# Column-normalised attention folded into a two-layer MLP: scores in two row halves, single-block first tiles, and GpSimd in the sum of squares

## Chip, core and metric

The kernel runs on one core of one Trainium2 chip. The metric is device time in microseconds (us) of one launch; the kernel before was timed in three runs, with a median of 1041.66 us (1041.51 to 1043.06).

## The reference, cut to what is computed

```python
def _attn_ref(q, k, v, tau):                     # q, k, v: (1, 6016, 256) float32
    qn = q / (np.linalg.norm(q, axis=1, keepdims=True) + 1e-06)
    kn = k / (np.linalg.norm(k, axis=1, keepdims=True) + 1e-06)
    s = kn.transpose(0, 2, 1) @ qn / tau          # 256 x 256: channels against channels
    s = s - s.max(-1, keepdims=True)
    a = np.exp(s)
    a /= a.sum(-1, keepdims=True) + 1e-09
    return (v @ a).astype(np.float32)

def _moe_ref(x, w_in, w_out):                     # w_in 256 x 2048, w_out 2048 x 256, float64
    h = x @ w_in
    g = h * (1.0 / (1.0 + np.exp(-1.702 * h)))
    return (g @ w_out).astype(np.float32)

def _moe2_ref(x, w_in, w_out):
    h = x @ w_in
    return (np.maximum(0.01 * h, h) @ w_out).astype(np.float32)
# out = _moe2_ref(_moe_ref(_attn_ref(q, k, v, tau), moe weights), moe2 weights)
```

## The kernel before

The norms run over the 6016 rows, so the attention is a 256 x 256 matrix of scores between channels, and a softmax over its rows. The kernel never forms v @ a: it folds a into the first layer's weights (`fold`, L478) and multiplies v by those. Exact float32 products are made of three float32r products (`terms`, L88): each operand is split into a high and a low part (`halves`, L94: ScalarE copies the high part, VectorE subtracts), and high x high, high x low and low x high are added up. The weights come as float64 words and are turned into float32 by a chain of small steps, `convert` (L193), driven by a generator: each `go_on(n)` (L296) emits the next n steps, so it is the place of `go_on` in the program that places this work in the queues of VectorE and ScalarE.

The whole order is written out by hand: each engine executes its instructions in the order of the program.

1. Front (L301 to L404). q and k come in tiles of `rows` (L318: 1, 1, 2, ten times 4, 2 and 1 blocks of 128 rows), eight tiles ahead, q on SP's DMA queue and the first three tiles of k on ScalarE's. Six small products `warm` (L370) precede them. For each block the TensorE makes both halves of the scores, `s_ps[kc]`, one product of 256 columns each, with q as the weights, so that the rows of the scores are channels of q. ScalarE squares the tile and VectorE adds the squares into `acc` (`add_squares`, L343). `norms` (L354) sums `acc` over the partitions ahead of the last three blocks' products.
2. Chain (L417 to L475). The inverse norms of q and tau go into two diagonal matrices `dq`; ScalarE copies the scores (`st`), and eight instructions at L442 multiply the transposed scores by `dq`. Then a row maximum, `Exp` with the inverse norm of k as its scale, four transposes at L463, and the split of the exponentials into `eth` and `etl`.
3. First block of v (L406 to L504 and L666 to L704). `transpose_v` turns v's first 1024 rows, `fold(0)` makes the first slice of folded weights `wa[0]`, and `hidden_first` makes the hidden products of slice f, for both 512-row halves u and for both w_in halves s; `emit_y` multiplies the activated tiles by `wo`, one pair of tiles behind.
4. The remaining blocks and the second layer (`step`, L706, and `last_step`, L763), at a steady pace that the change doesn't touch.

PSUM has eight banks: y00, y10, y01, y11 and h0 to h3. A bank is used under several names one after the other, and a new use waits for the readers of the old one: `nrm` is h0, `et` is h1, the scores are y00 and y10, and `hidden_first` writes bank h(2s+u).

Of the kernel before, what the change touches and what calls it, by code (L numbers as in the profile page):

```python
# [7 lines left out]
F32 = mybir.dt.float32  # L8
# [9 lines left out]
def tile_kernel(  # L18
# [31 lines left out]
    P = 128  # L50
# [28 lines left out]
    ones = small(const, 1, "ones")  # L79
# [34 lines left out]
    with tc.manual_schedule():  # L114
# [15 lines left out]

        make_identity(nc, ident)
        nc.gpsimd.memset(ones, 1.0)
# [60 lines left out]
        def convert(key):  # L193
# [28 lines left out]
            if name == "wo":  # L222
                hi, lo = (wo[f][:, s].rearrange("p k c -> p (k c)") for s in range(2))
                nc.vector.tensor_copy(hi, flat)
                yield
                subtract(lo, flat, hi.bitcast(F32))
                yield
                return
            if name == "wi":
                wi = early.tile([P, 2, BLK], F32R, tag="ws", name="wi", bufs=2)  # L230
                nc.vector.tensor_copy(wi[:, 0], flat)
                yield
                subtract(wi[:, 1], flat, wi[:, 0].bitcast(F32))
                ready[f] = wi
                yield
                return
# [66 lines left out]
        sc = front.tile([P, KC, C], F32, name="sc")  # L303
        taub = small(front, 1, "taub")
        rtau = small(front, 1, "rtau")
        dq = front.tile([P, KC, P], F32, name="dq")
        root = small(front, 4, "root")
        rr = small(front, 4, "rr")
        rn = small(front, 4, "rn")
        mx = small(front, KC, "mx")  # L310
        rk = small(front, KC, "rk")
        st = front.tile([P, KC, C], F32, name="st")
        den = small(early, KC, "den")
        rden = small(early, KC, "rden")
        nc.vector.memset(acc, 0.0)


        rows = [1, 1, 2] + [4] * 10 + [2, 1]  # L318
# [19 lines left out]
        V_TILE = 7  # L338
        CONVERT = {last - 1: 5}
# [3 lines left out]
        def add_squares(j):  # L343
            t, n = qk(j), rows[j]
            sq = front.tile([P, 2, 4, C], F32, tag="sq", name="sq", bufs=2)
            nc.scalar.activation(out=sq[:, :, :n, :], in_=t[:, :, :n, :], func=AF.Square)
            step = 2 if j < last - 1 else 1
            for r in range(0, n, step):
                m = min(step, n - r)
                add(acc[:, :, :m, :], acc[:, :, :m, :], sq[:, :, r:r + m, :])  # L350
            if j == last - 2:
                add(acc[:, :, 0, :], acc[:, :, 0, :], acc[:, :, 1, :])

        def norms():  # L354
            for i in range(2):
                for kc in range(KC):
                    nc.tensor.matmul(  # L357
                        nrm[:, 2 * i + kc:2 * i + kc + 1],
                        lhsT=acc[:, i, 0, kc * P:(kc + 1) * P],
                        rhs=ones,  # L360
                        start=True,
                        stop=True,
                    )

        for j in range(AHEAD):
            load_qk(j)
            if j == 2:
                nc.scalar.preload_act_table(AF.Sqrt)

        warm = bank("h3")  # L370
        for _ in range(6):
            nc.tensor.matmul(warm[:, :P], lhsT=ident, rhs=ident, start=True, stop=True)
        for j in range(len(rows)):
            t, n = qk(j), rows[j]
            if j == last - 1:

                for i in range(last - 1, last + 1):
                    add_squares(i)
                norms()
            for r in range(n):  # L380
                for kc in range(KC):
                    nc.tensor.matmul(  # L382
                        s_ps[kc][:, :C],
                        lhsT=t[:, 0, r, kc * P:(kc + 1) * P],
                        rhs=t[:, 1, r, :],
                        start=(j == 0 and r == 0),
                        stop=(j == last and r == n - 1),
                    )
            if j < last - 1:
                add_squares(j)  # L390
            go_on(CONVERT.get(j, 0))
            if j + AHEAD <= last:
                load_qk(j + AHEAD)
            if j == V_TILE:
                for _ in range(3):
                    next_load()
# [6 lines left out]
            if j == last - 1:  # L403
                nc.vector.reciprocal(out=rtau, in_=taub)  # L404

        def transpose_v(c, tags):  # L406
            pts = [bank(tag) for tag in tags]
            for kc in range(KC):
                for i in range(BLK // P):
                    nc.tensor.transpose(  # L410
                        pts[kc][:, i * P:(i + 1) * P],
                        qk(V_TILE)[:, c, i, kc * P:(kc + 1) * P], ident,
                    )
            return pts


        nc.vector.tensor_scalar_add(rr, nrm[:, 0:4], 1e-35)  # L417
# [13 lines left out]

# [3 lines left out]
        for d in range(KC):  # L435
            nc.scalar.copy(st[:, d, :], s_ps[d][:, :C])
        go_on(2)

        sq_ps = [bank("h2"), bank("h3")]
        for kc in range(KC):  # L440
            for d in range(KC):
                nc.tensor.matmul(  # L442
                    sq_ps[kc][:, d * P:(d + 1) * P],
                    lhsT=st[:, d, kc * P:(kc + 1) * P], rhs=dq[:, d, :], start=True, stop=True,
                )
        vt0 = transpose_v(0, ("y01", "y11"))

        for kc in range(KC):
            row = sq_ps[kc][:, :C]
            nc.vector.tensor_reduce(out=mx[:, kc:kc + 1], in_=row, axis=AX.X, op=ALU.max)  # L450
            nc.vector.tensor_scalar(
                out=mx[:, kc:kc + 1], in0=mx[:, kc:kc + 1], scalar1=rk[:, kc:kc + 1], scalar2=-1.0,
                op0=ALU.mult, op1=ALU.mult,
            )
            nc.scalar.activation(  # L455
                out=sc[:, kc, :], in_=row, func=AF.Exp, bias=mx[:, kc:kc + 1],
                scale=rk[:, kc:kc + 1], accum_out=den[:, kc:kc + 1],
            )
        go_on(2)
        et = bank("h1")  # L460
        for kc in range(KC):
            for d in range(KC):
                nc.tensor.transpose(  # L463
                    et[:, d * C + kc * P:d * C + (kc + 1) * P], sc[:, kc, d * P:(d + 1) * P], ident
                )
        et3 = et.rearrange("p (d c) -> p d c", d=KC)
        nc.vector.tensor_copy(eth, et3)  # L467
        subtract(etl, et3, eth.bitcast(F32))
        nc.vector.tensor_scalar_add(rden, den, 1e-9)
        nc.vector.reciprocal(out=rden, in_=rden)  # L470
        for dst, src in ((xa[0], vt0[0]), (xbt, vt0[1])):
            halves(dst[:, 0, 0], dst[:, 1, 0], src)
        nc.scalar.preload_act_table(AF.Gelu_apprx_sigmoid)
        while 0 not in ready:
            go_on(1)  # L475


        def fold(f):  # L478

            wi = ready.pop(f).rearrange("p h (d n) -> p h d n", d=KC)  # L480
            pw = bank("h0" if f == 1 else "h3").rearrange("p (k n) -> p k n", k=KC)
            for kc in range(KC):
                c0 = slice(kc * P, (kc + 1) * P)
                for d in range(KC):
                    terms(pw[:, kc], (eth[:, d, c0], etl[:, d, c0]), (wi[:, 0, d], wi[:, 1, d]),
                          d == 0, d == KC - 1)
            raw = early.tile([P, 4, P], F32, tag="tp", name="raw")
            for kc in range(KC):

                nc.scalar.activation(  # L490
                    out=raw[:, 0::3] if kc == 0 else raw[:, 1:3],
                    in_=pw[:, kc].rearrange("p (s n) -> p s n", s=2), func=AF.Copy,
                    scale=rden[:, kc:kc + 1],
                )
# [4 lines left out]

        fold(0)  # L500
        vt1 = transpose_v(1, ("y00", "y10"))
        for dst, src in ((xa[0], vt1[0]), (xbt, vt1[1])):
            halves(dst[:, 0, 1], dst[:, 1, 1], src)
        go_on(4)  # L504
# [161 lines left out]
        def hidden_first(f):  # L666
# [5 lines left out]
            for u in range(2):  # L672
                hp = bank(f"h{2 * s + u}")
                for kc, x in enumerate((xa[0], xbt)):
                    terms(hp, (wa[g][:, 0, at[kc]], wa[g][:, 1, at[kc]]),
                          (x[:, 0, u], x[:, 1, u]), kc == 0, kc == KC - 1)
                act(1, h[:, u], hp)
            if f == NF:
                fold(1)
# [12 lines left out]
        for f in range(NF):  # L692
            for s in range(2):
# [7 lines left out]
                emit_y(len(pend) - 2)  # L701
# [183 lines left out]
```

## Time and profile before

| | |
|---|---|
| median of three runs | 1041.66 us |
| the profiled execution, its time and its span | 1043.86 us, 1042.0 us |
| mean granted TensorE clock over the span | 0.997 |
| TensorE busy | 1031.5 us, 99% |
| VectorE, ScalarE, GpSimd busy | 775.0, 589.9 and 0.7 us |
| TensorE's first score product | 4.07 us |
| the norms' products | 46.84 us |
| first hidden product | 58.32 us |
| hidden products of slice 2, first half, and their y done | about 88.1 us |

In the profile PE is the TensorE's matrix products, DVE is VectorE, ACT is ScalarE, POOL is GpSimd and SP the engine that issues DMAs. A float32 product shows as two instructions, so one block's product with one half of the scores ("a unit" below) is two rows. The ends of matmuls are modelled, so short waits of the TensorE hide in their durations: its real pace is read from the starts. [...]

### The profile page before, as it was taken

Reading aid. Unit: us, or ns where it says so; the run is one execution under the profiler, and the core shown is the slowest. Engines: PE = TensorE matmul, PEld = TensorE weight load, DVE = VectorE, ACT = ScalarE, POOL = GpSimd, SP = SyncE. Lnnn points to the kernel's source line nnn. Section 1 sums busy time; section 2 is a strip of 40 time slices with the busy share of each in tenths; the row PEclk is TensorE's granted clock in tenths of the full one; section 3 lists DMA queues with packets and bytes.
Section 4 is the critical chain, followed back from the end, with each engine's and each line's share of the span. In section 5 each row is a group of like instructions: output and inputs, shape, how many; then the busy total and the mean of one; then the engine's idle time right before and its main releaser. Section 6 shows DMA issues by size and latency. Waiting matters only on the chain.

```text
span 1042.0 us, 12633 instructions
## 1 busy us (share of the span) xinstructions
PE 1031.5 (99%) x4676; PEld 870.6 (84%) x4676; DVE 775.0 (74%) x1187; ACT 589.9 (57%) x864; POOL 0.7 (0%) x7
## 2 busy tenths in 40 slices
PE   8999999999999999999999999999999999999998
PEld 7878888888888888888998888888888888888997
DVE  6889868888888888888766667577567667676655
ACT  5465555666556666666556555555555555455453
POOL 0000000000000000000000000000000000000000
PEclk9999999999999999999999999999999999999999
DMA  9646423015224223212744002101200300300202
GB/s 361 234 126 167 129 65 91 10 31 150 92 68 110 98 76 103 89 56 96 263 167 152 1 1 42 41 1 19 63 1 9 73 1 1 76 1 1 41 1 36
DMA packets 120077, 81.82 MB, mean 79 GB/s; under 512 B 93392, under 2 KB 104400, under 8 KB 118736
## 3 DMA queue, kind: packets, MB, share of 16 engines
q1 hardware_dynamic: 115872, 80.04, 25.3%
q10 hardware_dynamic: 4144, 0.98, 0.4%
q8 instruction: 36, 0.59, 0.2%
q14 instruction: 25, 0.20, 0.1%
HBM read 55.05 MB, written 25.95 MB: 78 GB/s over the span
## 4 chain that ended last, share of the span: by engine, by line
PE 97%; DVE 1%; DMA 1%; issue 0%; ACT 0%; ACTq 0%; DVEq 0%
PE y L92 49%; PE h L92 44%; PE y L382 4%; DMA qk<-in_k_dram 1%; DVE gd L99 0%; PE h L442 0%; ACTq L330 0%; ACT raw L490 0%; ACT sc L455 0%; DVE ta L208 0%; PE h L357 0%; DVE ta L203 0%; DVE etl L99 0%; DVE eth L467 0%; DVE ta L212 0%
## 5 line engine op out<-in xcount | busy, mean ns | idle before, releaser
L92 PE MATMUL y<-gd,wo 128*128 128x512 f32 (+1 forms) x1248 | 296.5, 386 | 0.1
L92 PE MATMUL h<-xa,wa 128*128 128x512 f32 (+1 forms) x1152 | 276.5, 385 | 0.5 <-DVE wa L496 0.5
L92 PEld LDWEIGHTS y<-gd,wo 128*128 128x128 f32 x1248 | 233.8, 188 | 44.1 <-DVE gd L99 0.4
L92 PEld LDWEIGHTS h<-xa,wa 128*128 128x128 f32 x1152 | 216.2, 188 | 41.7 <-DVE wa L496 0.8
L92 PE MATMUL y<-g,wo 128*128 128x512 f32 (+1 forms) x1044 | 246.8, 385 | 0.0
L92 PEld LDWEIGHTS y<-g,wo 128*128 128x128 f32 x1044 | 196.0, 188 | 36.3
L92 PE MATMUL h<-xb,wa 128*128 128x512 f32 (+1 forms) x888 | 217.3, 385 | 0.0
L92 PEld LDWEIGHTS h<-xb,wa 128*128 128x128 f32 x888 | 166.7, 188 | 31.1
L99 DVE TENSOR_TENSOR tv<-tp,h 128x512 f32<-128x512 f32 (+1 forms) x88 | 59.3, 674 | 114.4 <-PE h L92 111.8
L99 DVE TENSOR_TENSOR cc<-tv,h 128x512 f32<-128x512 f32 (+1 forms) x176 | 116.0, 673 | 34.9 <-PE h L92 34.4
L96 DVE TENSOR_TENSOR gd<-cc,gd 128x1024 fp32r<-128x1024 f32 (+1 forms) x87 | 104.1, 1197 | 0.0
L722 ACT COPY tp<-h 128x512 f32<-128x512 f32 (+1 forms) x87 | 50.4, 580 | 93.2 <-PE h L92 92.6
L95 ACT CAST gd<-cc 128x1024 fp32r<-128x1024 f32 (+1 forms) x87 | 90.0, 1035 | 0.0
L516 ACT ACTIVATE cc<-cc 128x1024 f32<-128x1024 f32 (+2 forms) x49 | 50.3, 1027 | 38.9 <-DVE cc L99 38.9
L516 ACT ACTIVATE tt<-tt 128x512 f32<-128x512 f32 (+1 forms) x48 | 30.0, 625 | 72.4 <-DVE tt L99 72.4
L99 DVE TENSOR_TENSOR tt<-tv,h 128x512 f32<-128x512 f32 (+1 forms) x88 | 59.4, 675 | 9.9 <-DVE tv L99 0.9
L99 DVE TENSOR_TENSOR tt<-tt,h 128x512 f32<-128x512 f32 (+1 forms) x88 | 59.4, 675 | 9.2
L514 ACT ACTIVATE cc<-cc 128x1024 f32<-128x1024 f32 (+1 forms) x40 | 41.6, 1041 | 40.9 <-DVE cc L99 40.9
L99 DVE TENSOR_TENSOR g<-tt,g 128x512 fp32r<-128x512 f32 (+1 forms) x87 | 58.6, 673 | 7.2 <-ACT g L733 6.9
L514 ACT ACTIVATE tt<-tt 128x512 f32<-128x512 f32 (+1 forms) x40 | 24.9, 623 | 64.8 <-DVE tt L99 64.8
L99 DVE TENSOR_TENSOR g<-tp,g 128x512 fp32r<-128x512 f32 (+1 forms) x87 | 58.6, 674 | 0.0
L746 ACT CAST g<-tp 128x512 fp32r<-128x512 f32 (+1 forms) x87 | 53.2, 612 | 2.8
(97 smaller groups left out, 713.0 us busy)
## 6 DMA issues: line engine op xcount, KB each, us to landing
cv<-in_moe_w_in_dram SPq DMA_DIRECT2D x32, 256.0 KB, 3.2
cv<-in_moe_w_out_dram SPq DMA_DIRECT2D x16, 512.0 KB, 3.9
wa<-w2a SPq DMA_DIRECT2D x8, 896.0 KB, 4.7
qk<-in_q_dram SPq DMA_DIRECT2D x10, 512.0 KB, 9.9
qk<-in_k_dram SPq DMA_DIRECT2D x10, 512.0 KB, 10.0
x<-stg SPq DMA_DIRECT2D x5, 1024.0 KB, 4.6
stg<-x SPq DMA_DIRECT2D x5, 1024.0 KB, 5.2
out_dram<-o SPq DMA_DIRECT2D x80, 64.0 KB, 1.9
```

Of the source, the lines that this page charges most:

```text
L92: nc.tensor.matmul(dst, lhsT=w, rhs=x, start=start, stop=stop, skip_group_check=more)
L95: nc.scalar.copy(hi, raw)
L96: nc.vector.tensor_tensor(out=lo, in0=raw, in1=hi.bitcast(F32), op=ALU.subtract)
L99: nc.vector.tensor_tensor(out=out, in0=in0, in1=in1, op=op)
L382: nc.tensor.matmul(s_ps[kc][:, :C], lhsT=t[:, 0, r, kc * P:(kc + 1) * P], rhs=t[:, 1, r, :], start=(j == 0 and r == 0), stop=(j == last an ...
L514: nc.scalar.activation(out=out, in_=in_, func=AF.Gelu_apprx_sigmoid)
L516: nc.scalar.activation(out=out, in_=in_, func=AF.Prelu, alpha=0.01)
L722: nc.scalar.copy(tp, pa)
L746: nc.scalar.copy(g11[:, 0], tp)
```

## The change

- Tiles: six tiles of one block, one of two, nine of four, then two and one. Four tiles of k instead of three go by ScalarE's queue. The small products ahead multiply `ones` (now 128 x 128, set before `ident`) instead of `ident`.
- Squares: in the tiles of four blocks up to tile 14 VectorE adds three blocks and GpSimd the fourth, into an accumulator `accp` of its own (eight such adds). The last three tiles are squared and added q and k apart, then `accp` and the second half of `acc` are added in.
- Scores: k is the weight operand, so rows are channels of k. Tiles 0 to 13 make both halves; tiles 14 to 17 (11 blocks) only half 0 before the norms. The 11 products of half 1 come after the norms, in groups of 2, 4, 3 and 2 between the steps of the chain.
- Chain: instead of the copies `st` and the products at L442, `spread` sends the scaled inverse norms of q to all partitions with one product by `ones`; one VectorE instruction multiplies a half of the scores by it and takes the maximum. The chain runs once for each half. `fold(0)`, its scaling and its split are done by halves as well, and the first products of slice 0 on the first 128 channels of v (`first_products(0, ...)`) are put among them.
- Slice 0 of the first block: only the second 128 channels are left in `hidden_first`; its y products come right after the hidden products of both s (no longer one pair behind), with `fold(1)` between them.
- The high parts of `wi` 0 and 1 and of `wo` 0 are copied by ScalarE instead of VectorE.

The diff, cut to its core:

```diff
-    ones = small(const, 1, "ones")
+    ones = const.tile([P, P], F32, name="ones")
...
+        nc.gpsimd.memset(ones, 1.0)
         make_identity(nc, ident)
-        nc.gpsimd.memset(ones, 1.0)
...
-                nc.vector.tensor_copy(hi, flat)
+                (nc.scalar.copy if f == 0 else nc.vector.tensor_copy)(hi, flat)
...
-                nc.vector.tensor_copy(wi[:, 0], flat)
+                (nc.scalar.copy if f < 2 else nc.vector.tensor_copy)(wi[:, 0], flat)
...
-        rows = [1, 1, 2] + [4] * 10 + [2, 1]
+        nc.gpsimd.memset(accp, 0.0)
+        rows = [1] * 6 + [2] + [4] * 9 + [2, 1]
...
-                eng = nc.scalar if j < 3 and i == 1 else nc.sync
+                eng = nc.scalar if j < 4 and i == 1 else nc.sync
...
-        V_TILE = 7
-        CONVERT = {last - 1: 5}
+        V_TILE = 10
+        LATE = last - 3
...
+        def squares(j, i):
+            t, n = qk(j), rows[j]
+            sq = front.tile([P, 2, 4, C], F32, tag="sq", name="sq", bufs=2)
+            nc.scalar.activation(out=sq[:, i, :n, :], in_=t[:, i, :n, :], func=AF.Square)
+            for r in range(0, n, 2):
+                m = min(2, n - r)
+                add(acc[:, i, :m, :], acc[:, i, :m, :], sq[:, i, r:r + m, :])
...
+                    nc.tensor.matmul(
+                        s_ps[h][:, :C],
+                        lhsT=t[:, 1, r, h * P:(h + 1) * P],
+                        rhs=t[:, 0, r, :],
...
+        for j in range(LATE + 1):
             t, n = qk(j), rows[j]
...
+            scores(j, range(KC) if j < LATE else (0,))
+            sq = front.tile([P, 2, 4, C], F32, tag="sq", name="sq", bufs=2)
+            nc.scalar.activation(out=sq[:, :, :n, :], in_=t[:, :, :n, :], func=AF.Square)
+            for r in range(0, min(n, 3), 2):
+                m = min(2, min(n, 3) - r)
+                add(acc[:, :, :m, :], acc[:, :, :m, :], sq[:, :, r:r + m, :])
+            if n == 4:
+                nc.gpsimd.tensor_tensor(out=accp, in0=accp, in1=sq[:, :, 3, :], op=ALU.add)
...
+        for j in range(LATE + 1, last + 1):
+            for i in range(2):
+                squares(j, i)
+        add(acc[:, :, 0, :], acc[:, :, 0, :], accp)
+        add(acc[:, :, 0, :], acc[:, :, 0, :], acc[:, :, 1, :])
+        for j in range(LATE + 1, last + 1):
+            scores(j, (0,))
+        go_on(4)
+        norms()
...
+        def spread():
+            nc.tensor.matmul(
+                nrm[:, C:2 * C], lhsT=ones, rhs=dq.rearrange("p k c -> p (k c)"),
+                start=True, stop=True,
+            )
+            nc.scalar.copy(rq, nrm[:, C:2 * C])
...
+        def softmax(h):
+
+            nc.vector.tensor_tensor_reduce(
+                out=sc[:, h], in0=s_ps[h][:, :C], in1=rq, scale=rk[:, h:h + 1],
+                scalar=-3.0e38, op0=ALU.mult, op1=ALU.max, accum_out=mx[:, h:h + 1],
+            )
...
+        transpose_v(0, ("h1", "h2"))
+        split_v(0, 0)
+        second_half(2)
+        spread()
+        go_on(1)
+        softmax(0)
+        split_v(0, 1)
+        second_half(4)
+        et = bank("h3")
+        turn(0)
+        split_e(0)
+        second_half(3)
+        wi0 = ready.pop(0)
+        raw0 = early.tile([P, 4, P], F32, tag="tp", name="raw")
+        pw0 = [bank(tag)[:, :C] for tag in ("y01", "y11")]
+        fold_products(pw0[0], wi0, 0)
+        second_half(len(late_rows))
+        transpose_v(1, ("y00", "h1"))
+        softmax(1)
+        fold_scale(raw0, pw0[0], 0)
+        fold_half(raw0, 0, 0)
...
+        first_products(0, [(0, 0)])
+        turn(1)
+        split_e(1)
+        split_v(1, 0)
+        first_products(0, [(1, 0)])
+        fold_products(pw0[1], wi0, 1)
+        fold_scale(raw0, pw0[1], 1)
+        split_v(1, 1)
         nc.scalar.preload_act_table(AF.Gelu_apprx_sigmoid)
...
+        fold_half(raw0, 0, 1)
+        nc.sync.dma_start(out=w1raw[0], in_=raw0)
+        first_products(0, [(0, 1), (1, 1)])
+        go_on(5)
...
+                if g == 0:
+                    hp = hp0[s, u]
+                    first_products(1, [(s, u)])
...
-            if f < 2 * NF - 1:
+            if 0 < g and f < 2 * NF - 1:
                 go_on(4)
             subtract(gd[:, 1], h, gd[:, 0].bitcast(F32))
+            if g == 0:
+                go_on(4)
...
-                emit_y(len(pend) - 2)
+                if f == 0 and s == 0:
+                    continue
+                if f == 0:
+                    emit_y(2)
+                    fold(1)
+                    emit_y(2)
+                    fetch()
+                else:
+                    emit_y(len(pend) - 2)
```

## Rows read from the trace of the kernel before

**Rows 1.** The page: busy time of each engine; shares of the chain that ended last.
```profile
PE 1031.5 (99%) x4676; PEld 870.6 (84%) x4676; DVE 775.0 (74%) x1187; ACT 589.9 (57%) x864; POOL 0.7 (0%) x7
...
PE 97%; DVE 1%; DMA 1%; issue 0%; ACT 0%; ACTq 0%; DVEq 0%
```

**Rows 2.** Waits of TensorE, whole span: total us, times, longest.
```profile
PE y L382 <- DMA qk<-in_k_dram: 2.2, 1, 2.2
PE h L372 <- POOL ones L132: 1.3, 1, 1.3
```

**Rows 3.** Timeline of TensorE, 0 to 60 us: start, us, engine, line, instructions, [idle before].
```profile
4.07 2.53 PE L382 MATMUL y<-qk 128*128 128x256 f32 x8
8.85 38.16 PE L382 MATMUL y<-qk 128*128 128x256 f32 x168 [2.25 <-DMA qk<-in_k_dram]
46.84 0.95 PE L357 MATMUL h<-ones,acc 128*128 128x1 f32 x8
...
56.77 1.03 PE L410 MATMUL y<-ident,qk 128*128 128x128 f32 x8
```

**Rows 4.** Stretches: PE, PEld, DVE, ACT, POOL busy (instructions), granted clock, DMA share, GB/s.
```profile
8.00:9.00 1.00, 0.15 (x1) 0.16 (x1) 0.00 (x0) 0.13 (x1) 0.00 (x0) 0.88 1.03 412
9.00:10.00 1.00, 1.00 (x3) 0.82 (x4) 0.04 (x1) 0.93 (x1) 0.00 (x0) 0.50 1.03 418
...
10.00:15.00 5.00, 5.00 (x20) 4.21 (x19) 2.97 (x3) 3.22 (x2) 0.00 (x0) 0.78 1.02 419
```

**Rows 5.** The DMA view of 0 to 9 us: what was moved.
```profile
DMA packets 1189, 2.27 MB, mean 252 GB/s; under 512 B 123, under 2 KB 635, under 8 KB 1189
```

**Rows 6.** Timelines of ScalarE and VectorE, 0 to 70 us: the squares and their sums.
```profile
3.44 1.35 ACT L346 ACTIVATE sq<-qk 128x512 f32<-128x512 f32 x2
...
13.18 25.79 DVE L99 TENSOR_TENSOR acc<-acc,sq 128x1024 f32<-128x1024 f32 x20 [1.99 <-ACT sq L346]
...
39.80 2.21 DVE L99 TENSOR_TENSOR acc<-acc,sq 128x512 f32<-128x512 f32 x3
```

**Rows 7.** Groups by line and shape, 0 to 80 us: busy us, mean ns | idle before.
```profile
L99 DVE TENSOR_TENSOR acc<-acc,sq 128x1024 f32<-128x1024 f32 x21 | 25.7, 1225 | 7.7 <-ACT sq L346 6.4
L346 ACT ACTIVATE sq<-qk 128x2048 f32<-128x2048 f32 x10 | 19.1, 1913 | 6.7 <-DMA qk<-in_k_dram 3.5 <-DVE acc L99 3.2
...
L99 DVE TENSOR_TENSOR acc<-acc,sq 128x512 f32<-128x512 f32 x5 | 3.5, 692 | 2.5 <-ACT sq L346 2.2
...
masks.py:199 POOL TENSOR_SCALAR_AFFINE_SELECT ident<-ident 128x128 f32<-128x128 f32 x1 | 0.3, 292 | 0.1
```

**Rows 8.** Timeline of VectorE, 0 to 70 us: two steps of the chain after the norms.
```profile
47.82 0.16 DVE L417 TENSOR_SCALAR rr<-h 128x4 f32<-128x4 f32 x1 [2.68 <-PE h L357]
...
49.15 0.60 DVE L427 TENSOR_SCALAR dq<-ident,rn,rtau 128x128 f32<-128x128 f32 x2
```

**Rows 9.** Groups by line and shape, 0 to 80 us: steps of chain and first block.
```profile
L680 ACT CAST gd<-h 128x1024 fp32r<-128x1024 f32 x4 | 4.2, 1058 | 0.1
...
L99 DVE TENSOR_TENSOR gd<-h,gd 128x1024 fp32r<-128x1024 f32 x3 | 3.7, 1218 | 0.0
...
L490 ACT ACTIVATE raw<-h,rden 128x256 f32<-128x256 f32 x6 | 2.5, 472 | 0.7 <-PE h L92 0.7
...
L455 ACT ACTIVATE sc<-h,mx,rk 128x256 f32<-128x256 f32 x2 | 1.1, 564 | 1.3 <-DVE mx L451 1.3
```

**Rows 10.** Timeline of all engines, 57 to 92 us: fold(1), first and a later y.
```profile
64.17 0.40 PE L92 MATMUL h<-wi,eth 128*128 128x256 f32 x2
...
65.61 3.32 PE L92 MATMUL y<-gd,wo 128*128 128x512 f32 x12
...
85.34 2.91 PE L92 MATMUL y<-gd,wo 128*128 128x512 f32 x12
```

**Rows 11.** The chain that ended last, in order of time: twelve hidden products.
```profile
75.91 2.72 PE h L92 x12
```

**Rows 12.** Stretches, columns as in rows 4: the first block's later slices.
```profile
100.00:110.00 10.00, 10.00 (x51) 8.52 (x50) 9.66 (x18) 4.62 (x7) 0.00 (x0) 1.00 0.39 133
```

More of the change, by code (lines that the diff above doesn't have):

```diff
@@ L371, in tile_kernel @@
         for _ in range(6):
-            nc.tensor.matmul(warm[:, :P], lhsT=ident, rhs=ident, start=True, stop=True)
-        for j in range(len(rows)):
+            nc.tensor.matmul(warm[:, :P], lhsT=ones, rhs=ones, start=True, stop=True)
+        for j in range(LATE + 1):
             t, n = qk(j), rows[j]
[L375 to L391, printed above, removed]
+            scores(j, range(KC) if j < LATE else (0,))
[6 more added lines that the diff above has]
+                nc.gpsimd.tensor_tensor(out=accp, in0=accp, in1=sq[:, :, 3, :], op=ALU.add)
             if j + AHEAD <= last:
@@ L402, in tile_kernel @@
                     )
[L403 to L417, printed above, removed]
+                for _ in range(2):
+                    next_load()
+        for j in range(LATE + 1, last + 1):
[7 more added lines that the diff above has]
+        norms()
+        nc.vector.reciprocal(out=rtau, in_=taub)
+        nc.vector.tensor_scalar_add(rr, nrm[:, :4], 1e-35)
         nc.scalar.activation(out=root, in_=rr, func=AF.Sqrt)
@@ new lines, in tile_kernel, with transpose_v, split_v @@
+        vt = {}
+        def transpose_v(kc, tags):
+            for u, tag in enumerate(tags):
+                vt[kc, u] = bank(tag)
+                for i in range(BLK // P):
+                    nc.tensor.transpose(
+                        vt[kc, u][:, i * P:(i + 1) * P],
+                        qk(V_TILE)[:, u, i, kc * P:(kc + 1) * P], ident,
+                    )
+        def split_v(kc, u):
+            dst = xbt if kc else xa[0]
+            halves(dst[:, 0, u], dst[:, 1, u], vt[kc, u])
@@ L454, in tile_kernel, with turn @@
             )
             nc.scalar.activation(
[L456 to L461 removed]
+                out=ex[:, h], in_=sc[:, h], func=AF.Exp, bias=nmx[:, h:h + 1],
+                scale=1.0, accum_out=den[:, h:h + 1],
+            )
+        def turn(h):
             for d in range(KC):
                 nc.tensor.transpose(
[L464 removed]
+                    et[:, h * C + d * P:h * C + (d + 1) * P], ex[:, h, d * P:(d + 1) * P], ident
@@ L465, in tile_kernel, with split_e @@
                 )
[L466 to L472, printed above, removed]
+        def split_e(h):
+            cols = slice(h * P, (h + 1) * P)
+            src = et[:, h * C:(h + 1) * C].rearrange("p (d c) -> p d c", d=KC)
+            nc.scalar.copy(eth[:, :, cols], src)
+            subtract(etl[:, :, cols], src, eth[:, :, cols].bitcast(F32))
+            nc.vector.tensor_scalar_add(rden[:, h:h + 1], den[:, h:h + 1], 1e-9)
+            nc.vector.reciprocal(out=rden[:, h:h + 1], in_=rden[:, h:h + 1])
@@ new lines, in fold_half, with second_half @@
+        def fold_half(raw, f, kc):
+            at = slice(0, 4, 3) if kc == 0 else slice(1, 3)
+            hi, lo = wa[f][:, 0, at], wa[f][:, 1, at]
+            nc.vector.tensor_copy(hi, raw[:, at])
+            subtract(lo, raw[:, at], hi.bitcast(F32))
+        late_rows = [(j, r) for j in range(LATE, last + 1) for r in range(rows[j])]
+        def second_half(count):
+            for j, r in late_rows[:count]:
+                scores(j, (1,), (r,))
+            del late_rows[:count]
+        transpose_v(0, ("h1", "h2"))
```

102 lines of the change are left out of this document (47 added, 55 removed).

## The prediction, as it was put on record

> **What bounds the kernel now.** First the page: the TensorE is busy 99% of the span and is 97% of the chain that ended last [rows 1]. So the change can win only where the TensorE waits, runs at its lower clock or does work that is dropped, and it loses where it makes new waits. The view of its waits names two large ones, both at the start: 1.3 us for `ones` and 2.2 us for the third k tile [rows 2]. Its timeline shows the second as a hole before 8.85 us [rows 3], and the stretches behind it show what else that cost: the granted clock is 0.88, then 0.50, and 0.78 as a mean over 10 to 15 us [rows 4]. [...]
>
> Paces I need. [...] A 512-column product: 2.72 / 12 = 0.227 us [rows 11]. A fold product: twelve from 64.17 to 65.61 us, 0.12 [rows 10]. A transpose (line 410): 0.13 [rows 3].
>
> The sum runs from the norms (N) to the end of the y behind the hidden products of slice 2, first half, where both kernels have the same work behind them. Before: 46.84 us [rows 3] to 85.34 + 2.72 = 88.06 us [rows 10], 41.2 us. Its work: norms 0.8, 6 units 2.6, the products at line 442 1.2, 16 transposes 2.1, 4 turns 0.5, 48 fold products 5.8, 60 hidden and 48 y products 24.5: 37.5 us. So 3.7 us are waits, part of them inside modelled durations.
>
> **Part 1: until the norms.** Removed: the hole and the clock loss. `ones` no longer waits for GpSimd's two steps on `ident`, and the first tile is there by 3.44 us, when its square starts [rows 6], so the first unit can start at 3.7 instead of 4.07. The first two blocks took 2.53 us instead of 1.73 [rows 3], partly a slow start; I keep 0.5 of it. Do tiles keep up? 8 blocks are needed by 3.7 + 0.5 + 8 x 0.864 = 11.1 us, and the ninth tile of work is a four-block tile: 12 blocks are 3.15 MB; before, 2.27 MB were in by 9 us [rows 5] at 418 GB/s behind that [rows 4], so 3.15 MB by 11.1 us. I take 0.2 us of waits. The fourth k tile on ScalarE's queue puts that engine's table load and first square back by one issue, which nobody waits for. SP's queue passes one weight piece instead of three before v, so v is earlier. Then N = 3.7 + 0.5 + 83 units x 0.432 + 0.2 = 40.3 us, against 46.84: 6.5 us earlier, of which 2.2 are the five units not yet made.
>
> Squares must be done by then. Before, VectorE had added them by 42.0 us [rows 6] and waited. Now the first four-block tile is squared by about 11.2 + 1.9 [rows 7] = 13.1 us, later ones come each 2.5 us (1.05 MB at 419 GB/s [rows 4]), and VectorE needs 1.225 + 0.69 = 1.92 us [rows 7] for each, so it follows the data: tile 14 is added at about 32.5 us. The last three tiles cost six adds of 0.69 and two of some 0.4, the two merges 1.4: 6.4 us, done at 39.3. That is 1 us ahead of N, if GpSimd takes nothing from VectorE. The four steps of `go_on(4)` (1.8 us of VectorE) then stand ahead of `rr`; the norms' products cover half of it.
>
> GpSimd's add isn't in the trace. Bounds: no less than VectorE's 0.69 us for the same shape; its one pass over 128 columns took 0.292 us [rows 7], four times that is 1.2. By itself either fits under 2.5 us. What it does to VectorE beside it no row shows: nothing, or it shuts VectorE out while it runs. I take nothing, because N then hangs on the TensorE with 1 us to spare; the other end is a rival.
>
> **Part 2: the chain.** Work dropped: line 442, 1.2 us. Added: `spread` 0.43; 11 units instead of 6 after N, 2.2 us. Work +1.4. Waits, walked through in each engine's order (+0.05 to a hand-over, 0.25 from a product's start to its reader), from N:
> - `dq` is done 2.9 us after N, as before (46.84 to 49.75 [rows 3, 8]); norms, eight transposes and 2 units fill 2.7: **0.3**.
> - `spread`, ScalarE's copy 0.4, the new multiply-and-maximum (not in the trace; 0.43 to 0.69 by VectorE's rows of 256 and 512 columns, I take 0.6), 0.2, `Exp` 0.56 [rows 9], with v's subtract and `wi`'s subtract ahead of it on VectorE: 6.1; 4 units fill to 5.1: **0.9**.
> - `turn`, 3 units, six fold products, 2 units, eight transposes reach 10.2. The first hidden product waits for `wa`, whose split is queued behind the second half's maximum and `Exp`: 9.4 + 0.6 + 0.2 + 0.56 + 0.2 + 0.47 [rows 9] + 0.28 and hand-overs = 11.9: **1.7**.
> - Two products' worth, `turn` and six fold products reach 14.35. The next hidden product writes bank h1, which the last part of v leaves only after fold scaling 0.47, copy 0.6 and subtract 0.67: **2.0**.
> - Slice 0's y now comes right behind its six remaining hidden groups. ScalarE is held by `wo`'s new copy, then two Gelu of 0.6 and the high-part copy of 1.06 [rows 9]: **1.1**, and the low part 1.22 [rows 9] behind that, with one product to fill it: **1.0**. Before, the hidden products of the other half stood there.
> - `fold(1)` waits for `wi` 1: **0.4**; the second pair's high and low parts: **0.2** and **1.0**; slice 1, with no y between: **0.4** and, for bank h3, **0.6**.
>
> Together 9.6 us, against 3.7: +5.9. VectorE's three casts of 0.43 that ScalarE took over cost 0.6 each there; they are in these steps. Behind slice 2 both kernels run alike; VectorE is 97% busy there [rows 12], so it gives nothing back, and the four fewer conversion steps by then are paid later beside TensorE work.
>
> **Sum.** -6.5 + 1.4 + 5.9 = +0.8 us on the profiled span; by the same walk on the kernel before my steps come out about 0.2 us long, so +0.6. The profiled execution was 1043.86 us, 2.2 above the median; I carry the difference to the median: 1041.66 + 0.6 = 1042.3 us. "No change" is within 0.2%, 2.1 us, about what a measurement of this kernel can tell.
>
> **Rivals.**
> 1. *The chain waits no longer than before* (faster). The units stand exactly where the chain needs cover, half-size steps are shorter, and if the 9.6 us shrink to 3.7 to 6.5 the result is 1036.4 to 1039.2. For it: my largest waits are sums of six to nine steps, each rounded up; the multiply-and-maximum may be 0.4. Against: the bank h1 wait and the y of slice 0 come from the order alone, whatever the durations.
> 2. *GpSimd's adds hold up VectorE's* (slower). If the two can't run at once, a tile costs 1.92 + 0.69 to 1.2 = 2.6 to 3.1 us, 3.2 with hand-overs, not 2.5. Eight tiles from 13.1 end at 34.5 to 38.7, the rest 6.4 later: 41 to 45 us; plus 0.6 for the conversion steps then bare ahead of `rr`. N moves by 1 to 5.5 us and the result is 1043.5 to 1048. It decides from 2.9 us per tile (N over 42.5). For it: both engines read the same tile just as ScalarE releases it. Against: no row shows the two slowing each other. [...]
> [...]
> 4. *The single-block tiles don't come earlier* (the change doesn't do what it says): more, smaller transfers on the same queues. If the hole and the low clock stay, N is 3.9 us later: 1046.
>
> **How the numbers follow.** Forecast 0.36 (1040.5 to 1043.7), rival 1 0.32, rival 2 0.20, rival 3 0.07, rival 4 0.05. Faster by over 0.2%: rival 1, 0.32. Within 0.2%: the forecast and the low end of rival 2, 0.38. Slower: 0.30. The range leaves out the far halves of rivals 1 and the last of rival 2: 1037.8 to 1047.5 us.
>
> **What would show it.** Right: no hole of the TensorE over 0.5 us before 12 us, and a clock of 1.00 from about 5 us; norms at 40 to 41 us; waits for `wa` and bank h1 of 1.5 to 2 us some 10 and 14 us after N; two of about 1 us before slice 0's y. Rival 1 shows as waits of under 6 us in all from the norms on. Rival 2 shows as adds of `acc` above 1.225 us or gaps between them beside GpSimd's, and a wait of the norms' products for VectorE. [...] Wrong in another way: an `accp` add of over 2.5 us, which would hold the squares' buffers, or a wait behind 88 us that the kernel before doesn't have.

## The result, and the profile after

The changed kernel takes 1053.0 us (median of four runs, 1052.71 to 1053.49) against 1042.2 us: a ratio of 1.0104, 95% interval 1.0086 to 1.0121. That is 10.8 us slower, where 0.6 us was forecast, and outside the range. The profiled execution has a span of 1051.2 us, against 1042.0.

The page of the changed kernel first: busy times, and shares of the chain that ended last, to be held against [rows 1].

```profile
PE 1034.0 (98%) x4670; PEld 871.6 (83%) x4670; DVE 779.1 (74%) x1196; ACT 593.3 (56%) x874; POOL 13.4 (1%) x16
...
PE 93%; DVE 3%; DMA 1%; ACT 1%; issue 1%; SPq 0%; ACTq 0%; DVEq 0%
```

VectorE's share of the chain has gone from 1% to 3%, and the page puts 2.7% of the span down to one line, the sums into `acc`: some 28 us in which the squares, not the TensorE, set the end. The TensorE's waits of the whole span (total, times, longest) name the place:

```profile
PE h L369 <- DVE acc L99: 3.7, 1, 3.7
PE y L357 <- DMA qk<-in_k_dram: 2.4, 2, 1.8
PE h L92 <- DVE xb L96: 1.9, 1, 1.9
PE y L92 <- DVE gd L99: 1.5, 2, 0.8
PE h L92 <- DVE wa L507: 1.2, 1, 1.2
```

Line 369 is the norms' product. Its timeline (start, us, what, [idle before]):

```profile
3.71 6.69 PE L357 MATMUL y<-qk 128*128 128x256 f32 x24
11.02 1.97 PE L357 MATMUL y<-qk 128*128 128x256 f32 x8 [0.61 <-DMA qk<-in_k_dram]
14.78 29.16 PE L357 MATMUL y<-qk 128*128 128x256 f32 x134 [1.80 <-DMA qk<-in_k_dram]
47.66 1.87 PE L369 MATMUL h<-ones,acc 128*128 128x1 f32 x8 [3.72 <-DVE acc L99]
```

The scores are through at 43.94 us (14.78 + 29.16), then the TensorE stands for 3.7 us, because the last squares are added only at 47.6. The eight products behind the wait take 1.87 us instead of 0.95 [rows 3]: the clock has fallen. The stretches 44 to 45 and 47 to 54 us (columns as in [rows 4]):

```profile
44.00:45.00 1.00, 0.00 (x0) 0.00 (x0) 0.86 (x2) 0.79 (x2) 0.00 (x0) 1.00 0.00 0
...
47.00:54.00 7.00, 6.34 (x23) 5.80 (x24) 5.21 (x15) 2.66 (x5) 0.00 (x0) 0.52 0.25 78
```

Now the squares. First VectorE's sums into `acc` by shape between 16 and 46 us (busy us, mean ns | idle before), to be read beside [rows 7]; then four of GpSimd's eight adds on its timeline, and two of VectorE's adds beside them:

```profile
L99 DVE TENSOR_TENSOR acc<-acc,sq 128x1024 f32<-128x1024 f32 x8 | 13.8, 1726 | 4.1 <-ACT sq L389 3.4
L99 DVE TENSOR_TENSOR acc<-acc,sq 128x512 f32<-128x512 f32 x14 | 13.4, 966 | 0.6
```

```profile
24.68 1.26 POOL L394 TENSOR_TENSOR accp<-accp,sq 128x512 f32<-128x512 f32 x1 [1.00 <-ACT sq L389]
28.62 1.28 POOL L394 TENSOR_TENSOR accp<-accp,sq 128x512 f32<-128x512 f32 x1 [2.68 <-ACT sq L389]
30.68 1.43 POOL L394 TENSOR_TENSOR accp<-accp,sq 128x512 f32<-128x512 f32 x1 [0.78 <-ACT sq L389]
34.80 1.28 POOL L394 TENSOR_TENSOR accp<-accp,sq 128x512 f32<-128x512 f32 x1 [2.69 <-ACT sq L389]
...
24.80 1.69 DVE L99 TENSOR_TENSOR acc<-acc,sq 128x512 f32<-128x512 f32 x1
28.65 2.34 DVE L99 TENSOR_TENSOR acc<-acc,sq 128x1024 f32<-128x1024 f32 x1
```

VectorE's add of 1024 columns takes 1.73 us instead of 1.225, that of 512 on average 0.97 instead of 0.69, and GpSimd's starts repeat every two tiles, 34.80 - 28.62 = 6.18 us: 3.09 us a tile. Before it was 25.79 us for twenty adds [rows 6], 2.58 a tile. VectorE was given a quarter less to add and takes longer for it. The single adds show where: the two at 24.80 and 28.65 us begin just after one of GpSimd's and take 1.00 and 1.11 us longer than alone, while those at 26.59 and 27.85 us, with GpSimd idle, keep 1.23 and 0.69. That both engines read the same tile is not needed: in the order of the squares the add at 24.80 still belongs to the third four-block tile, and GpSimd's at 24.68 reads the fourth.

From the norms on, I measure to the start of the y behind slice 2's first hidden products, where the work behind is the same. In the changed kernel that y is

```profile
95.08 2.91 PE L92 MATMUL y<-gd,wo 128*128 128x512 f32 x12
```

against 85.34 us before [rows 10]: 9.7 us later; the span is 9.2 us longer, so half a microsecond is made up behind it. Of the 9.7, 0.8 are ahead of the norms (47.66 against 46.84 [rows 3], though with five units less done, so 3.0 for equal work) and 8.9 behind (47.4 us against 38.5).

### The profile page after: what moved, and what is told of

It reads as the page before. It is cut to its first block, busy times and chain, and to the rows that moved or that the text cites. A ratio compares the mean times of both kernels' runs of the same rounds, so it can differ in the third digit from the quotient of the medians.

```text
span 1051.2 us, 12671 instructions
## 1 busy us (share of the span) xinstructions
PE 1034.0 (98%) x4670; PEld 871.6 (83%) x4670; DVE 779.1 (74%) x1196; ACT 593.3 (56%) x874; POOL 13.4 (1%) x16
## 4 chain that ended last, share of the span: by engine, by line
PE 93%; DVE 3%; DMA 1%; ACT 1%; issue 1%; SPq 0%; ACTq 0%; DVEq 0%
PE y L92 49%; PE h L92 43%; DVE acc L99 3%; DMA qk<-in_k_dram 1%; PE h L493 1%; PE y L357 1%; ACT h L586 0%; ACT gd L754 0%; ACT sq L389 0%; PE h L369 0%; PE h L450 0%; PE y L493 0%; DVE ta L212 0%; DVE ta L208 0%; DVE gd L99 0%
## 5 line engine op out<-in xcount | busy, mean ns | idle before, releaser
L588 ACT ACTIVATE cc<-cc 128x1024 f32<-128x1024 f32 (+2 forms) x49 | 50.3, 1027 | 38.9 <-DVE cc L99 38.9
## 6 DMA issues: line engine op xcount, KB each, us to landing
qk<-in_k_dram SPq DMA_DIRECT2D x9, 512.0 KB, 10.2
```

The lines of the kernel that those rows point to most:

```text
L588: nc.scalar.activation(out=out, in_=in_, func=AF.Prelu, alpha=0.01)
```

## The experiments

All times are medians beside runs of the kernel before on the same chip, which gave 1042.1 to 1042.4 us. Theory A was formed from the profile above: GpSimd's adds and VectorE's shut each other out. Theory B was its rival: the sums are late because the tiles are.

**e1: GpSimd's adds undone.**

```diff
-            for r in range(0, min(n, 3), 2):
-                m = min(2, min(n, 3) - r)
+            for r in range(0, n, 2):
+                m = min(2, n - r)
...
-            if n == 4:
-                nc.gpsimd.tensor_tensor(out=accp, in0=accp, in1=sq[:, :, 3, :], op=ALU.add)
...
-        add(acc[:, :, 0, :], acc[:, :, 0, :], accp)
```

> The changed kernel with one part undone: VectorE adds all four blocks of each tile's squares, GpSimd adds none and accp is gone. Theory A (GpSimd's adds and VectorE's two-input adds shut each other out): VectorE falls back from about 3.08 us to 2.58 us per four-block tile, its sums end near 43.5 us instead of 47.6, the norms' products start when the TensorE comes to them, at 43.9 to 44.2 us, the wait of 3.7 us and the half clock behind it go, and the time falls from 1053.0 to about 1047.5 us. Theory B (the sums are late only because the tiles are late, and GpSimd takes work off VectorE as meant): VectorE has 0.69 us more to add in each of eight tiles, the norms come at 48 to 51 us, and the time stays at 1053 or rises to 1056 us.

Measured: 1047.69 us, ratio 1.0054 (1.0040 to 1.0067): 5.3 us back. Timeline of the TensorE, two lines, and groups of the sums, 0 to 50 us:

```profile
42.94 0.95 PE L367 MATMUL h<-ones,acc 128*128 128x1 f32 x8
...
89.29 2.91 PE L92 MATMUL y<-gd,wo 128*128 128x512 f32 x12
```

```profile
L99 DVE TENSOR_TENSOR acc<-acc,sq 128x1024 f32<-128x1024 f32 x17 | 20.8, 1225 | 5.8 <-ACT sq L387 4.9
L99 DVE TENSOR_TENSOR acc<-acc,sq 128x512 f32<-128x512 f32 x12 | 8.1, 690 | 4.4 <-ACT sq L387 3.7
```

With more to add, VectorE is done 4.8 us earlier (42.8 instead of 47.6), every add at its old length, and the norms' products wait for nobody and run at full clock (0.95 us for the eight instead of 1.87; 1.00 from 43 to 54 us). The sums and the time are those of theory A, and B falls. This kernel is also the clean view of the rest: norms at 42.94 us, and 46.35 us from there to the y, 7.85 more than before. Its waits of the TensorE from 40 to 100 us:

```profile
PE h L92 <- DVE xb L96: 1.9, 1, 1.9
PE h L433 <- DVE dq L424: 1.7, 1, 1.7
PE y L92 <- DVE gd L99: 1.5, 2, 0.8
PE h L92 <- DVE wa L502: 1.2, 1, 1.2
PE y L92 <- ACT gd L749: 0.7, 1, 0.7
PE h L92 <- ACT raw L493: 0.2, 1, 0.2
```

**e2: GpSimd's adds alone, put into the kernel before.** Their sum is read by nobody.

```diff
+            if n == 4:
+                nc.gpsimd.tensor_tensor(out=accp, in0=accp, in1=sq[:, :, 3, :], op=ALU.add)
             step = 2 if j < last - 1 else 1
```

> The kernel before with one addition: for each of the ten four-block tiles GpSimd adds the fourth block's squares into a scratch tile that nothing reads; VectorE's work stays as it was. Theory A (the two shut each other out): each four-block tile costs VectorE some 1.3 us more than its 2.58, its adds show 1.6 us and more instead of 1.23 beside GpSimd's, the sums end 10 to 13 us later than 42 us, the norms come at 51 to 55 us instead of 46.84, and the time rises by 5 to 10 us to 1047 to 1052 us. Theory B (they run side by side): adds of 1.23 us, norms at 46.8 us, 1042 us.

Measured: 1051.13 us, ratio 1.0086 (1.0072 to 1.0100). Groups of both engines, 0 to 60 us, and the norms:

```profile
L99 DVE TENSOR_TENSOR acc<-acc,sq 128x1024 f32<-128x1024 f32 x21 | 35.1, 1674 | 6.9 <-ACT sq L348 5.6
L350 POOL TENSOR_TENSOR accp<-accp,sq 128x512 f32<-128x512 f32 x10 | 15.7, 1567 | 28.0 <-ACT sq L348 28.0
```

```profile
50.97 1.84 PE L361 MATMUL h<-ones,acc 128*128 128x1 f32 x8 [5.54 <-DVE acc L99]
```

VectorE's work is the same, instruction for instruction, and its twenty-one adds take 35.1 us instead of 25.7 [rows 7]: 0.94 us more for each of GpSimd's ten, where 1.3 was expected. The time rises by 8.7 us: the norms are late, and from them to the y it is 41.8 us (the y starts at 92.77) instead of 38.5, with a clock of 0.50 from 53 to 56 us. So much from ten instructions on an otherwise idle engine.

**e8: GpSimd as busy, but reading nothing.** Thirty-six memsets of a scratch tile in the kernel before.

```diff
+        scratch = front.tile([P, 1024], F32, name="scratch")
+        for _ in range(36):
+            nc.gpsimd.memset(scratch, 0.0)
```

> The kernel before, with GpSimd kept busy to about 38 us by 36 memsets of 128 x 1024 of a scratch tile, which read nothing from SBUF. If it is GpSimd's reads that shut VectorE's two-input adds out: adds of 1.23 us, norms at 46.8 us, 1042 us. If any GpSimd instruction does: adds of 1.5 us and more and norms later, 1045 us and more.

Measured: 1042.14 us in its one timed run. GpSimd's group, and VectorE's sums beside it, 0 to 45 us, then two lines of the TensorE's timeline:

```profile
L318 POOL MEMSET scratch<- 128x1024 f32 x36 | 34.3, 952 | 2.0
...
L99 DVE TENSOR_TENSOR acc<-acc,sq 128x1024 f32<-128x1024 f32 x21 | 25.7, 1225 | 6.6 <-ACT sq L349 5.3
...
8.78 36.53 PE L385 MATMUL y<-qk 128*128 128x256 f32 x168 [1.26 <-DMA qk<-in_k_dram]
45.15 0.95 PE L360 MATMUL h<-ones,acc 128*128 128x1 f32 x8
```

Neither GpSimd's being busy nor its writes cost the time. What is left of its adds is that they read SBUF beside VectorE's two-input adds; no run had GpSimd read without adding. Beside GpSimd's adds, which read, VectorE's adds of 1024 columns went from 1.225 to 1.67 us on average (e2); beside memsets, which only write, they stayed at 1.225 (e8). The price here is 0.94 us of VectorE for an add whose own shortest span is 1.26.

This run shows one thing more. It has the tiles of the kernel before, and its norms come at 45.15 us, not at 46.84 [rows 3]: its granted clock is 1.00 from 5 to 25 us, where the profiled execution of the kernel before fell to 0.50 behind its first hole [rows 4].

**e3: as e1, with the tiles of the kernel before.** What is left is the halves, the chain and the copies on ScalarE.

```diff
-        rows = [1] * 6 + [2] + [4] * 9 + [2, 1]
+        rows = [1, 1, 2] + [4] * 10 + [2, 1]
```

> As the run without GpSimd's adds, but with the tiles of the kernel before (1, 1, 2, ten times 4, 2, 1 blocks, three k tiles on ScalarE's queue, v after tile 7); halves, chain and the rest as in the changed kernel. If the single-block tiles are worth what the two traces say (8.0 blocks done by 14.8 us against 6.9, so 0.95 us), the norms come some 0.7 us later than without GpSimd's adds alone, at 44.7 us, and the time is about 1 us above that run, 1048.5 us. If the single-block tiles cost more than they bring (holes of 0.6 and 1.8 us before 14.8 us), it is below that run.

Measured: 1047.81 us, ratio 1.0052 (1.0038 to 1.0066). Norms at 44.25 us, 1.3 later than in e1, and the same time: the wait for `dq` behind the norms is 0.22 us instead of 1.71, which makes up what is lost ahead of them. So the single-block tiles are worth nothing here, and halves, chain and copies cost 5.4 us.

**e4: the tiles and the products on `ones` alone, in the kernel before.** The edit is the reverse of e3's line, four k tiles on ScalarE's queue, v after tile 10, and `ones` set first.

> The kernel before with the first part of the change alone: the new tiles (six of one block, one of two, nine of four, two, one), four k tiles on ScalarE's queue, v after tile 10, and the products ahead on ones. If the single-block tiles bring 0.95 us and nothing else hangs on them: norms at 45.9 us and 1041.2 us. If they bring nothing: 1042.2 us.

Measured: 1042.82 us, ratio 1.0014 (1.0005 to 1.0023): the tiles bring nothing here either. Its times spread from 1042.27 to 1045.45 us. The profiled one is among the shortest:

```profile
10.58 1.97 PE L382 MATMUL y<-qk 128*128 128x256 f32 x8 [0.39 <-DMA qk<-in_k_dram]
14.34 31.32 PE L382 MATMUL y<-qk 128*128 128x256 f32 x144 [1.79 <-DMA qk<-in_k_dram]
45.49 0.95 PE L357 MATMUL h<-ones,acc 128*128 128x1 f32 x8
```

The hole of 2.25 us has become several, the largest ahead of the first four-block tile. They vary: with these tiles it was 1.80, 1.59, 1.79, 0.98, 0.80 and 2.01 us in six profiled kernels. The five longest of e4's eleven executions, from 1043.77 us, have mean granted clocks of 0.997 and 0.998; of the six shorter ones four have 0.999 or 1.000. So the long ones are likely executions in which a hole costs the clock as well, but no profile here caught one.

**e7: other tiles in the kernel before.** Two-block instead of single-block tiles.

```diff
-        rows = [1, 1, 2] + [4] * 10 + [2, 1]
+        rows = [1, 1, 2, 2, 2] + [4] * 9 + [2, 1]
```

> The kernel before with other tiles alone: 1, 1, 2, 2, 2, nine times 4, 2, 1 blocks, four k tiles on ScalarE's queue, v after tile 8. If the hole of 2.25 us and the low clock behind it come from four-block transfers that share the DMA engines with the third k tile, two-block tiles bring that tile forward: hole under 1 us, clock 1.00, norms at 44.5 to 45.5 us and 1040 to 1041 us. If it is the number of bytes that lie ahead of it, the hole stays and the time is 1042.4 us.

Measured: 1041.35 us, ratio 0.9992 (0.9983 to 1.0001). Stretches and timeline:

```profile
5.00:10.00 5.00, 3.58 (x16) 2.83 (x15) 1.81 (x3) 2.00 (x3) 0.00 (x0) 1.00 1.02 398
...
8.09 36.50 PE L382 MATMUL y<-qk 128*128 128x256 f32 x168 [1.42 <-DMA qk<-in_q_dram]
44.43 0.95 PE L357 MATMUL h<-ones,acc 128*128 128x1 f32 x8
```

One hole of 1.42 us, more than the 1 us expected, a clock of 1.00 behind it, 398 GB/s from 5 to 10 us where the changed kernel's tiles move 275, and norms 2.4 us earlier than in the profile before (0.7 earlier than in e8). The y mark is 1.5 us earlier and the time 0.8 to 1.0: part is given back in the chain, which takes 39.4 us from the norms to the y (83.85) where it was 38.5, in an execution with a mean granted clock of 0.998. With `ones` first as well (e11) the time is the same.

> The kernel before with the tiles 1, 1, 2, 2, 2, nine times 4, 2, 1 (1041.35 us) and the products ahead on ones instead of ident, which starts the TensorE 0.36 us earlier. If that carries through, 1041.0 us; if the first tiles' arrival sets the pace to about 8 us, no difference from 1041.35 us.

e11 measured 1041.41 us, ratio 0.9992 (0.9983 to 1.0000): the earlier start of the products brought nothing (norms at 44.71 us, 44.43 in e7), so the first tiles' arrival sets the pace. These two are the best kernels of the study, by less than can be called more than no change.

**e5: slice 0's y one pair behind again (from e1).** Theory C: the rest of the loss is waits that the order makes. Theory D: VectorE behind the chain sets the pace anyway.

```diff
-                if f == 0 and s == 0:
-                    continue
-                if f == 0:
-                    emit_y(2)
-                    fold(1)
-                    emit_y(2)
-                    fetch()
-                else:
-                    emit_y(len(pend) - 2)
+                emit_y(len(pend) - 2)
...
+            if f == NF:
+                fold(1)
             nc.scalar.copy(gd[:, 0], h)
```

> The run without GpSimd's adds, with one more part undone: slice 0's y products come one pair of tiles behind again, and fold(1) among the hidden products, as in the kernel before. Theory C (the rest of the loss is waits that the order of the chain makes, and this order is one): the waits for gd of 0.7, 0.76 and 0.77 us and the 0.24 us for bank h3 go, and the time falls from 1047.7 by 2 to 2.5 us to about 1045.3 us. Theory D (behind the chain VectorE is 97% busy and sets the pace, so waits there are made up for later): the time stays at 1047.7 us, and waits for VectorE appear between 75 and 110 us.

Measured: 1051.45 us, ratio 1.0089 (1.0075 to 1.0103): 3.8 us slower than e1, where both theories had it faster or the same. The waits for `gd` are gone, and another stands in their place. The second line is the product behind the wait for bank h1, the third the same product in e1:

```profile
PE h L488 <- ACT wi L231: 4.1, 1, 4.1
...
61.44 2.89 PE L92 MATMUL h<-xa,wa 128*128 128x512 f32 x6 [1.86 <-DVE xb L96]
...
59.81 1.63 PE L92 MATMUL h<-xa,wa 128*128 128x512 f32 x6 [1.86 <-DVE xb L96]
```

`fold(1)` needs `wi` 1, which is converted behind slice 0's low part; the y products had hidden that. The changed kernel's order of y is not a mistake by itself: it fits conversion steps that come late. But not all of the 3.8 us is the order. Behind the same wait of 1.86 us the granted clock was 0.66 from 60 to 65 us in e5, and it fell once more behind the 4.1 us, to 0.67 from 70 to 75. By the granted clock these two stretches lost some 3.4 us of full-rate time in e5's profile (an estimate: the sum of what the clock is short of 1.00). e1's profiled execution has a mean of 1.000, and its six products behind the wait took 1.63 us instead of 2.89.

**e6: as e5, and v's last quarter is split ahead of the second half's fold products.**

```diff
+        split_v(1, 1)
         fold_products(pw0[1], wi0, 1)
         fold_scale(raw0, pw0[1], 1)
-        split_v(1, 1)
```

> As the run before it (slice 0's y one pair behind, no GpSimd adds), and the split of v's last quarter is emitted ahead of the second half's fold products, so that bank h1 is free earlier. Theory C: the wait of 1.86 us for bank h1 falls to at most 0.3 us, and the time to about 1043.5 us. Theory D: no change against that run.

Measured: 1049.36 us, ratio 1.0072 (1.0057 to 1.0088), 2.1 us below e5. The wait for bank h1 falls from 1.86 to 1.02 us, not to 0.3, and the time stays far from the 1043.5 us expected. The norms also came 1.5 us earlier in its profile (42.97 against 44.47), from the first tiles. From the norms to the y it is 47.6 us instead of 49.6: 0.8 of this is the shorter wait, the rest goes with a clock that stays at 1.00 behind it (55 to 65 us). The mean granted clocks of all executions agree (0.995 and 0.996 in e5's four, 0.996 and 0.997 in e6's), but they don't say why the clock fell in e5.

**e9: as e6, with the conversion steps placed where VectorE waits, and their high parts copied by VectorE again.**

```diff
-                (nc.scalar.copy if f == 0 else nc.vector.tensor_copy)(hi, flat)
+                nc.vector.tensor_copy(hi, flat)
...
-                (nc.scalar.copy if f < 2 else nc.vector.tensor_copy)(wi[:, 0], flat)
+                nc.vector.tensor_copy(wi[:, 0], flat)
...
-        go_on(4)
         norms()
...
+        go_on(2)
         spread()
-        go_on(1)
         softmax(0)
+        go_on(3)
         split_v(0, 1)
...
         split_e(0)
+        go_on(3)
         second_half(3)
...
         fold_half(raw0, 0, 0)
+        go_on(2)
```

> As e6 (no GpSimd adds, slice 0's y one pair behind, bank h1 freed earlier), and the conversion steps are placed anew: none ahead of the norms, wi 0 behind dq and around the first softmax, wo 0 where VectorE waits in the chain, wi 1 ahead of the hidden products; VectorE makes their high parts as in the kernel before. Theory C in its present form (the chain's loss is in where the conversion steps stand in VectorE's and ScalarE's queues, not in the halves as such): the wait for dq falls from 1.65 to under 0.3 us, the one for wi 1 at fold(1) from 4.4 to under 1 us, and the time from 1049.4 to 1043.5 to 1044.5 us. Theory E (the halves' chain itself is the longer one): the waits move to eth, wa and xb, and the time stays above 1046 us.

Measured: 1044.35 us, ratio 1.0022 (1.0012 to 1.0033): 5.0 us below e6 and 3.3 below e1. Its waits of the TensorE behind the first tiles:

```profile
PE h L92 <- DVE wa L501: 1.7, 1, 1.7
PE h L469 <- ACT ex L462: 1.0, 1, 1.0
PE h L92 <- DVE xb L96: 1.0, 1, 1.0
...
PE h L92 <- DVE wa L571: 1.0, 1, 1.0
PE h L432 <- DVE dq L423: 0.2, 1, 0.2
```

The wait for `dq` is 0.2 and that for `wi` 1 is gone, as expected; the two parts of the edit, the places and the engine of the copies, were not run apart. From the norms (43.73 us) to the y (86.50) it is 42.8 us, 4.3 more than before instead of 7.85. With the two-block tiles as well (e10) the time is 1042.83 us.

> As the run before it, with the tiles 1, 1, 2, 2, 2, nine times 4, 2, 1 blocks that gave 1041.35 us in the kernel before. If tiles and chain add up, it is about 1 us below that run, 1042.5 to 1043.5 us; under 1041 us it would be the best of all, which needs a chain no longer than that of the kernel before.

e10's ratio is 1.0007 (0.9998 to 1.0016). So the chain by halves, put in the best order I found, is still no shorter than the kernel before, and about 1.5 us longer than e7 with the same tiles.

## Why the prediction was wrong, point by point

1. **The step that failed** first is one sentence of part 1: "I take nothing, because N then hangs on the TensorE with 1 us to spare." GpSimd's adds cost VectorE 0.94 us each (e2) and the changed kernel 5.3 us (e1 against it). Rival 2 had the effect, its place, the 3.1 us per tile and a delay of the norms of 1 to 5.5 us; between e1 and the changed kernel it was 4.7. I gave it 0.20, and its upper end, 1048 us, still lies 5 us below the result, because point 3 comes on top. The only argument for "nothing" was that no row shows the two slowing each other, but no row could: the kernel before has no GpSimd instruction that reads SBUF beside a VectorE sum. Missing rows speak for neither end, and the margin was 1 us.
2. **Rivals were priced one at a time.** The 3.7 us wait that rival 2 makes is itself longer than the 2.25 us hole behind which the clock of the kernel before was 0.50 [rows 4], and a low clock came with it: 0.52 granted from 47 to 54 us. In e2, e5 and e6 waits of 5.5, 4.1 and 4.4 us are followed by low clock as well: 0.61 from 50 to 53 us, 0.67 and 0.81 from 70 to 75. Rival 3, at 0.07, was that the chain's own waits of 1.7 and 2.0 us bring the clock down, which would have made 1044 us, and there the traces differ: behind 1.86 us for bank h1 the clock stayed at 1.00 in the changed kernel (65 to 70 us) and in e1 (mean 1.000) and was 0.66 from 60 to 65 us in e5. Which of the shorter waits are followed by the low clock is not settled here.
3. **N at 40.3 us** would have been wrong without GpSimd too: 42.94 in e1. This is the second step that failed, "Removed: the hole and the clock loss", and it is nearly as large as the first. One term that was mis-sized is the arrival of the first four-block tile, 3.15 MB "by 11.1 us". It took the rate of four-block tiles; with single-block tiles less has been moved by 9 us than before (2.27 MB [rows 5]):

```profile
DMA packets 1930, 1.96 MB, mean 218 GB/s; under 512 B 208, under 2 KB 1744, under 8 KB 1930
```

   The packets under 2 KB are 1744 instead of 635, and SP issues k's seventh tile, the two-block one, only at 6.5 us; which of the two holds the tiles back was not run apart. The first four-block tile is there at 13.9 to 14.8 us. Rival 4 was half right: the tiles came no earlier on balance, but the hole became smaller ones at full clock. The 6.5 us gained ahead of the norms were 3.9 in e1's profile, 2.2 of them the five units put off, and the tiles gave nothing in the time (e3, e4).

   The other term is the clock loss, by [rows 4] 0.12 + 0.5 + 1.1 = 1.7 us of full-rate time, and with it the sentence "I carry the difference to the median". The profiled execution was 2.2 us above the median and had a mean granted clock of 0.997; of the 55 executions of the kernel before that were timed beside the experiments, 36 had 0.999 or 1.000. So a loss was counted as removable that the median execution mostly doesn't have. e8 shows it: same tiles, clock at 1.00, norms at 45.15 us. Against that, e1's 42.94 is 2.2 us earlier, which is the five units and nothing else. About 4.3 us of the miss (6.5 less 2.2) come from here, beside 5.3 from GpSimd. The 0.432 us of a unit in the sum for N, which stands in no row or run as such, did no harm: what the runs show is e8's 84 units in 36.53 us, 0.435 each.
4. **The chain** was right in size: 1.4 us of work and 5.9 of waits, 7.3 in all, against 7.85 measured in e1. By the prediction's own bookkeeping (46.35 + 2.72 us less 38.9 of work) e1 has 10.2 us of waits where 9.6 were added up; its view of waits names 7.3 of them, the rest is inside modelled durations. The named places were those walked through: bank h1 1.86 (predicted 2.0), `wa` 1.2 (1.7), the y of slice 0 0.71 and 0.76 (1.1 and 1.0), the second pair 0.77 (1.0), bank h3 0.24 (0.6). The wait for `dq` was 1.7 instead of 0.3, so that the sum fits this well is in part luck. Measured from the norms and against e3, where it is 0.22, `rr` comes 0.7 us later, because the conversion steps stand bare ahead of it once the norms come as soon as the sums are done, and the root 0.4 later still, behind ScalarE's copy of `wi`; a further 0.4 ahead of `dq` has no cause in the trace. I had written 0.6 of this into rival 2 alone. `turn` waited little in return. (The walk of the squares adds up to 38.9 us, not the 39.3 it gives; nothing hangs on it.)
5. **Rival 1** (waits no longer than before) found no support. And my reading that the bank and the y waits come "from the order alone" was too simple: undoing the y order alone cost 3.8 us, part of it clock (e5), since three orders (y, fold, conversions) hang together. Moving the conversions, with their copies back on VectorE, gave most: 5.0 us (e9).

The sum in hindsight, against the profile of the kernel before: tiles and earlier start -1.7 (norms of e1 for equal work), chain +7.85 less the 2.16 of units that it took over = +5.7, GpSimd with its clock +5.8: +9.7 before rounding, as measured at the y mark. Against e8, whose time is the median's, the first term is 0 and the sum 11.4 (95.08 against 83.66 us at the y mark), of which half a microsecond is made up behind it. On the clock of timed runs the same parts are about 0 (e3 against e1), +5.4 (e3 against before) and +5.3 (the changed kernel against e1), together 10.7 of 10.8. So the tiles' gain in the profiles is that of one long execution of the kernel before, and the medians don't have it.

## What to carry to other kernels

Before work goes to an idle engine, ask what it reads and what reads beside it: an add on GpSimd that read SBUF beside VectorE's two-input adds cost VectorE more (0.94 us) than the add that it took away (0.69). Where the trace can't show what two engines do to each other and the margin is as thin as here, one run with the new instruction alone and its result unused (e2) settles it. And when a chain is cut into halves to hide it, move every queue's other work, here the weight conversions, with it: the cover that the halves made on the TensorE was lost again, in part, to steps left standing in VectorE's queue.

## What the runs showed of the hardware that I had not expected

- GpSimd's add of 128 x 512 float32 took 1.26 us at its shortest, against VectorE's 0.69. VectorE's adds of 1024 columns beside it went from 1.225 to 1.73 us on average in the changed kernel and to 1.67 in e2; memsets of GpSimd left them at 1.225.
- A wait of 3.7 us of the TensorE was followed by a granted clock of 0.52 from 47 to 54 us. A wait of 1.86 us ahead of the same six products was followed by 0.66 from 60 to 65 us in e5, while e1's profiled execution has a mean of 1.000.
- From 5 to 10 us, the single-block tiles moved 275 GB/s in the changed kernel, the two-block tiles 398 in e7, and the tiles of the kernel before 382 in its own profile and 345 in e8.
